# Attention scores as 64-row products, one per head, in place of 128-row products against a zero-padded query

## The chip, the cores and the metric

The kernel runs on one core of one Trainium2 chip. The metric is device time in microseconds, from one launch that computes the whole output. The core has a matrix engine (TensorE, PE in the profile), a vector engine (DVE), a scalar engine (ACT), a general engine (POOL), a queue engine (SP) and 16 DMA engines; each compute engine works through its own list of instructions in order and waits on semaphores for the others.

## The reference

Causal attention over 4 batches, 8 heads, 768 positions and 64 channels a head, followed by a gated feed-forward block. Heads 0, 2 and 6 see all earlier keys; the other five see the first four keys (the sinks) and the last 64.

```python
scores = (1.0 / np.sqrt(D)) * np.matmul(q, k.transpose(0, 1, 3, 2))      # (4, 8, 768, 768), D = 64
rel = pos[:, None] - pos[None, :]
full_mask   = rel >= 0
stream_mask = (rel >= 0) & ((pos[None, :] < 4) | (rel < 64))
a = softmax(where(mask of the head, scores, -1e9))
attn_out = np.matmul(a, v)
x = attn_out.transpose(0, 2, 1, 3).reshape(B * S, H * D)                 # (3072, 512)
g = x @ w_gate                                                           # (3072, 1536)
out = (g * sigmoid(g) * (x @ w_val)) @ w_out                             # (3072, 512)
```

## The kernel before

The 3072 positions are cut into 24 tiles of 128 query rows (`TILES`, six to a batch; a tile's number inside its batch is `i`, its place in the run is `t`). Keys and queries are brought to channel-major form: `kT` holds, for each block of 128 keys, two heads one above the other in the 128 partitions, 64 channels each. `PAIRS` lists which heads share a block: (0, 2), (4, 6), (1, 3), (5, 7). `qT` is held twice, once with the lower 64 partitions zero and once with the upper 64 zero (`fill` writes the zeros in `qT`, and in `hqz` for the pairs that a DMA transposes). A product over all 128 partitions with one of these halves gives the score of one head alone.

For each tile, `plan` lists units of up to eight score blocks of 128 keys by 128 queries. A block is a pair number `p`, the heads of the pair that are wanted, a column `c` in the unit's score buffer, and a key block `kt`. A block wanted for both heads is one product of 256 columns: one weight load of the 128 by 128 key block, then both zero-padded queries streamed through it. A block wanted for one head is a product of 128 columns. The first two units of a tile with `i >= 1` hold eight blocks each (the diagonal block, the block before it and the sink block, for all heads as needed); the remaining units hold the older key blocks of the three full heads, 3(i-1) blocks in all. A tile with `i == 0` has one unit of eight.

`scores` issues a unit's products into `sc`, a buffer of eight blocks in two banks of the matrix engine's output memory; there is one such buffer. `exps` takes the exponential of the unit on ACT into `e`. From tile `LEAD = 4` on, the causal and window masks are multiplied into `e` afterwards by `mask` (DVE or POOL) from the constant tiles `m0`, `m1`, `m2`, which `mask_fills` writes once from `FILLS`. In the first four tiles the masks are added in the products instead. `values` multiplies `e` with the values (`av`, 65 columns a product, the last one for the row sum), `recip` and `norm` divide, and the result is transposed into `xt` (`xtranspose`, on PE for the first eight tiles, by a DMA afterwards). `gate` runs the gate and value products of the feed-forward (`gv`, 512 columns a product, four of them to a result), `tanh`, `stt1` and `stt2` form the hidden tile `h`, and `outproj` multiplies by the output weights (`o_ps`). `store` writes the rows.

The work of all tiles and of the feed-forward is one list of tasks, each a few instructions. Which engine takes a task is written out in `WAYS`, and the order in which all tasks are issued is written out in `ORDER`, two characters to a task; no scheduler decides either when the kernel is built. The last lines of the kernel go through it:

```python
    for number in P.order():
        if number < P.FILL:
            P.tasks[number].run()
```

So a unit of scores (`sc t.u`) stands between whatever feed-forward, value or transposing products the list has beside it.

Of the kernel before, what the change touches and what calls it, by code (L numbers as in the profile page):

```python
# [9 lines left out]
AF = mybir.ActivationFunctionType  # L10
# [95 lines left out]
def kernel(  # L106
# [42 lines left out]
    scale = 1.0 / (D ** 0.5)  # L149
# [18 lines left out]
    def buf(ring, shape, dt, name):  # L168
        return pools[ring].tile(shape, dt, name=name, tag=ring)
# [9 lines left out]
    def recast(task, dst, src):  # L179
        if task.way == "DVE":  # L180
            nc.vector.tensor_reduce(out=dst, in_=src.unsqueeze(len(src.shape)),  # L181
                                    axis=mybir.AxisListType.X, op=ALU.max)
        else:
            copy(task, dst, src)
# [13 lines left out]
        out=ident, in_=ident, compare_op=ALU.not_equal, fill=1.0,  # L198
# [12 lines left out]
    DIAG, BAND0, OWN, FAR = range(4)  # L211

    m0 = const.tile([128, 8, 128], FH, name="m0")
    m1 = const.tile([128, 4, 128], FH, name="m1")
    m2 = const.tile([128, 5, 128], FH, name="m2")
# [28 lines left out]
    def mask_fill(task, dst, src):  # L244
        src = nat[:, src].unsqueeze(1).to_broadcast([128, dst.shape[1], 128])
        if task.way == "ACT":
            nc.scalar.activation(out=dst, in_=src, func=AF.Identity, scale=-1.0 / OFF, bias=1.0)
        else:
            nc.vector.tensor_scalar(out=dst, in0=src, scalar1=-1.0 / OFF, op0=ALU.mult,
                                    scalar2=1.0, op1=ALU.add)  # L250

    def mask_fills(x):
        def run():
            for dst, src in FILLS[x]:
                mask_fill(T_fill[x], dst, src)
        return run

    FILLS = [[(m0[:, 0:4], BAND0), (m0[:, 4:6], DIAG), (m0[:, 6:7], BAND0), (m0[:, 7:8], DIAG),
              (m2[:, 1:4], DIAG), (m2[:, 0:1], OWN), (m1[:, 0:2], OWN)],
             [(m2[:, 4:5], FAR), (m1[:, 2:4], FAR)]]  # L260

    kT = [const.tile([128, NT, 2, 2, 128], FH, name=f"kT{n}") for n in range(2)]
    qT = [const.tile([128, 2, 4, 2, 128], FH, name=f"qT{n}") for n in range(2)]
# [106 lines left out]
    LEAD = 4  # L370
# [89 lines left out]
    def sinks_v(b, m):  # L460
        V = vt[b % 2]
        for j in range(2):
            rows = slice(j * 64, j * 64 + NSINK // 2)
            recast(T_sv[b, m], V[rows, m, STREAMS], V[rows, 0, STREAMS])

    def plan(t):


        b, i = TILES[t]
        if i == 0:  # L470
            if t == 0:
                return [([(p, (0, 1), 2 * x, 0) for x, p in enumerate(ps)], 4, None)
                        for ps in ((2, 3), (0, 1))]
            return [([(p, (0, 1), 2 * x, 0) for x, p in enumerate((2, 3, 0, 1))], 8, m0)]
        if t == 1:
            return [([(p, (0, 1), 0, i), (p, (0, 1), 2, -1)], 4, None) for p in (2, 3)] + [
                ([(1, (0, 1), 0, i), (0, (0, 1), 2, i)], 4, None),
                ([(1, (0,), 0, -1), (1, (1,), 1, 0), (0, (0, 1), 2, 0)], 4, None)]
        us = [([(2, (0, 1), 0, i), (2, (0, 1), 2, -1), (3, (0, 1), 4, i), (3, (0, 1), 6, -1)],
               8, m1),  # L480
              ([(1, (0, 1), 0, i), (0, (0, 1), 2, i), (1, (0,), 4, -1), (1, (1,), 5, 0),
                (0, (0, 1), 6, 0)], 8, m2)]
        rest = [(0, (0, 1), kt) for kt in range(1, i)] + [(1, (1,), kt) for kt in range(1, i)]
        unit, at = [], 0
        for p, hh, kt in rest:
            if at + len(hh) > 8:
                us.append((unit, at, None))
                unit, at = [], 0
            unit.append((p, hh, at, kt))
            at += len(hh)  # L490
        if unit:
            us.append((unit, at, None))
        return us

    def marks(t, u):

        if t >= LEAD:
            return []
        if t == 0:
            return [[(0, BAND0, 4)], [(0, DIAG, 2), (2, BAND0, 1), (3, DIAG, 1)]][u]  # L500
        if t == 1:
            return [[(0, OWN, 2), (2, FAR, 2)], [(0, OWN, 2), (2, FAR, 2)],
                    [(0, OWN, 1), (1, DIAG, 3)], [(0, FAR, 1)]][u]
        if TILES[t][1] == 0:
            return [(0, BAND0, 4), (4, DIAG, 2), (6, BAND0, 1), (7, DIAG, 1)]
        if u == 0:
            return [(0, OWN, 2), (2, FAR, 2), (4, OWN, 2), (6, FAR, 2)]
        return [(0, OWN, 1), (1, DIAG, 3), (4, FAR, 1)]

    def block(t, p, kt):  # L510

        b, i = TILES[t]
        kt = i - 1 if kt < 0 else kt
        return kT[b % 2][:, kt, p % 2, p // 2]

    def value(t, h, kt):
        b, i = TILES[t]
        kt = i - 1 if kt < 0 else kt
        return vt[b % 2][:, kt, slot(h), 0:65]

    whole_sc, es, av_blocks = {}, {}, {}

    def score_ring(t, u):
        return "gv" if t < 2 and u % 3 else "sc"

    def scores(t, u, unit):
        if t < 2:
            sc = [buf(score_ring(t, u), [128, 4, 128], FP, "sc")]
            whole_sc[t, u] = sc[0]
        else:  # L530
            sc = whole_sc[t, u] = buf("sc", [128, 8, 128], FP, "sc")
            sc = [sc[:, 0:4], sc[:, 4:8]]
        half = slice(t % 2 * 64, t % 2 * 64 + 64)
        terms = [(c, n, ident, nat[:, m].unsqueeze(1).to_broadcast([128, n, 128]))
                 for c, m, n in marks(t, u)]
        terms += [(c, len(hh), block(t, p, kt), qT[t // 2 % 2][:, hh[0]:hh[-1] + 1, p, :, half])
                  for p, hh, c, kt in unit[0]]
        for c, n, weights, moving in terms:
            first, last = True, True
            if t < LEAD:  # L540

                in_bank = [x for x in terms if x[0] // 4 == c // 4]
                first, last = moving is in_bank[0][3], moving is in_bank[-1][3]
            nc.tensor.matmul(  # L544
                sc[c // 4][:, c % 4:c % 4 + n, :], weights, moving, start=first, stop=last)

    def exps(t, u, unit):
        e = es[t, u] = buf("e", [128, 8, 128], FH, "e")
        for p, hh, c, kt in unit[0]:
            for n, s_ in enumerate(hh):  # L550
                h = PAIRS[p][s_]
                av_blocks.setdefault((t, h), []).append((e[:, c + n, :], value(t, h, kt)))
        n = unit[1]
        nc.scalar.activation(  # L554
            out=e[:, 0:n], in_=whole_sc.pop((t, u))[:, 0:n], func=AF.Exp, scale=scale)

    def mask(task, t, u, m):
        ev, mm = es[t, u][:, 0:m.shape[1]], m
        if m is m1:
            ev = es[t, u].rearrange("p (g n) q -> p g (n q)", g=2)  # L560
            mm = m.rearrange("p n q -> p (n q)").unsqueeze(1).to_broadcast([128, 2, 512])
        ENG[task().way].tensor_tensor(out=ev, in0=ev, in1=mm, op=ALU.mult)  # L562
# [121 lines left out]
    def tasks_of_tile(t):  # L684
        b, i = TILES[t]
        units = plan(t)
        n = t // 2
        k_deps = [x for kt in range(i // 2 + 1) for x in T_ev[QP.index((b, kt)), 2]]
# [9 lines left out]
        for u, unit in enumerate(units):  # L698
            mms, nb, m = unit
            streams = any(kt < 0 or kt == i for p, hh, c, kt in mms if p)  # L700
            added = [T_masks[0 if t == 0 else 1]] if t < LEAD else []
            sc = P.add(f"sc{t}.{u}", ["PE"], (lambda t=t, u=u, unit=unit: scores(t, u, unit)),
                       deps=k_deps + k_sinks + added, takes=[score_ring(t, u)])
            T_sc_of[b, i].append(sc)
            if streams:
                own.append(sc)
            ex = P.add(f"ex{t}.{u}", ["ACT"], (lambda t=t, u=u, unit=unit: exps(t, u, unit)),
                       deps=[sc], takes=["e"])
            P.uses(sc, score_ring(t, u), ex)
            ms = []  # L710
            if m is not None and t >= LEAD:
                cell = []
                ms.append(P.add(f"mask{t}.{u}", ["DVE", "POOL"],
                                (lambda cell=cell, t=t, u=u, m=m:
                                 mask(lambda: cell[0], t, u, m)), deps=[ex] + T_fill))
                cell.extend(ms)
            for p, hh, c, kt in mms:
                for s_ in hh:
                    hd = heads.setdefault(PAIRS[p][s_], [set(), set()])
                    hd[0].update(ms or [ex])  # L720
                    hd[1].add(ex)
# [206 lines left out]
```

The softmax here doesn't subtract the row's maximum and nothing guards it: scores larger than these inputs give would overflow.

## Time and profile before

| what | us |
|---|---|
| runs of the kernel | 257.55, 256.27, 257.90; median 257.55 |
| span of the profiled execution | 255.7 |
| PE busy by the profile | 246.3 (96%) |
| DVE / ACT / POOL busy | 172.8 / 140.8 / 83.0 |
| score products against the keys, L544 | 276, of which 196 of 256 columns and 80 of 128 |
| feed-forward products, L775 and L810 | 608 and 300 |
| products with the values, L574 | 472 |

The time that the runs give is the whole execution; the profiled one shows a span of 255.7 us from its first to its last instruction, and the median of the runs lies 1.85 us above that span. In the rows of the profile, "128*128" names the part of the array that a product takes, "128x256 f16" the streamed operand. A product's recorded duration runs from its start to its modelled end, and the records of neighbouring products overlap; so the durations of products can't be added up, and the pace of the engine is read from one start to the next. "PEld" is the row of weight loads. "sc", "av", "gv", "o_ps" are buffers that the products write.

### The profile page before, as it was taken

How to read it: one execution, taken by the hardware profiler on the slowest of the kernel's cores; microseconds unless marked ns; L12 is line 12 of the kernel's file. 1: busy time of each engine (PE TensorE's matmuls, PEld its weight loads, DVE VectorE, ACT ScalarE, POOL GpSimd, SP SyncE). 2: the span in 40 equal slices, each digit the busy share in tenths (PEclk: the TensorE clock that was granted, in tenths of full speed). 3: DMA queues.
4: the chain of work that ended last, by engine and by line, in shares of the span. 5: the costliest groups of instructions: out<-in, count | busy, mean ns of one | idle time of the engine just before them, and what ended most of it. 6: DMA issues, size and time to landing. Idle time of an engine off the chain costs nothing.

```text
span 255.7 us, 4837 instructions
## 1 busy us (share of the span) xinstructions
PE 246.3 (96%) x1812; PEld 137.0 (54%) x1812; DVE 172.8 (68%) x356; ACT 140.8 (55%) x218; POOL 83.0 (32%) x117
## 2 busy tenths in 40 slices
PE   7988999999999999999999999999999999999993
PEld 3566766665555564545565555455545544444442
DVE  4888899986978666776858776579674656454610
ACT  2488788777857673567786725644526322223111
POOL 7366666996670160044164361005000000000000
PEclk9999999999999999999999999999999999999999
DMA  6999999969999999999964962571200233103124
GB/s 186 290 312 332 319 327 322 295 194 198 343 196 223 233 218 164 248 217 201 185 139 93 306 156 38 104 145 42 62 0 3 62 85 82 41 0 82 44 68 99
DMA packets 80535, 42.52 MB, mean 166 GB/s; under 512 B 32768, under 2 KB 76032, under 8 KB 80512
## 3 DMA queue, kind: packets, MB, share of 16 engines
q1 hardware_dynamic: 80352, 42.09, 69.5%
q8 instruction: 14, 0.23, 0.4%
q10 hardware_dynamic: 160, 0.13, 0.2%
q14 instruction: 9, 0.07, 0.1%
HBM read 28.31 MB, written 6.29 MB: 135 GB/s over the span
## 4 chain that ended last, share of the span: by engine, by line
PE 81%; DVE 11%; ACT 2%; issue 2%; DMA 2%; POOL 0%; DVEq 0%; POOLq 0%; ACTq 0%
PE gv L775 43%; PE o_ps L810 22%; PE sc L544 9%; PE av L574 4%; DVE h L792 2%; PE warm L291 2%; ACT e L554 2%; DVE vt L181 2%; DMA xt<-xb 2%; DVE sil L785 1%; DVE xb L591 1%; DVE e L562 1%; DVE qT L177 1%; DVE o_sb L177 1%; DVE rc L579 1%
## 5 line engine op out<-in xcount | busy, mean ns | idle before, releaser
L554 ACT ACTIVATE e<-sc 128x1024 f16<-128x1024 f32 (+3 forms) x71 | 62.1, 879 | 35.4 <-PE sc L544 34.6
L775 PE MATMUL gv<-xt,wv_sb 128*128 128x512 f16 (+1 forms) x304 | 72.6, 368 | 1.0 <-DVE sil L785 0.9
L775 PE MATMUL gv<-xt,wg_sb 128*128 128x512 f16 (+1 forms) x304 | 71.7, 368 | 0.6 <-DMA xt<-xb 0.3
L781 ACT ACTIVATE sig<-gv 128x512 f32<-128x512 f32 (+1 forms) x76 | 43.2, 574 | 51.3 <-PE gv L775 47.5
L810 PE MATMUL o_ps<-wo_sb,h 128*128 128x512 f16 (+2 forms) x300 | 69.5, 370 | 0.0
L785 DVE SCALAR_TENSOR_TENSOR sil<-sig,gv 128x512 f32<-128x512 f32 (+1 forms) x76 | 48.9, 655 | 28.6 <-ACT sig L781 27.7
L792 DVE SCALAR_TENSOR_TENSOR h<-sil,gv 128x512 f16<-128x512 f32 (+1 forms) x76 | 48.9, 655 | 18.9 <-PE gv L775 17.3
L775 PEld LDWEIGHTS <-wv_sb 128*128 128x128 f16 x304 | 28.7, 98 | 28.7 <-issue 2.0
L810 PEld LDWEIGHTS <-h 128*128 128x128 f16 x300 | 28.2, 98 | 29.1
L775 PEld LDWEIGHTS <-wg_sb 128*128 128x128 f16 x304 | 28.8, 98 | 27.5 <-issue 0.8
L544 PE MATMUL sc<-qT,kT 128*128 128x256 f16 (+1 forms) x276 | 37.4, 257 | 0.2 <-DVE qT L177 0.2
L562 POOL TENSOR_TENSOR e<-e,m 128x640 f16<-128x640 f16 (+1 forms) x15 | 26.4, 1768 | 14.9 <-ACT e L554 10.7
L544 PEld LDWEIGHTS <-kT 128*128 128x128 f16 x276 | 24.7, 98 | 12.0 <-issue 1.3
L574 PEld LDWEIGHTS <-e 128*128 128x128 f16 x472 | 19.7, 97 | 9.5 <-DVE xb L591 1.8
L574 PE MATMUL av<-vt,e 128*128 128x65 f16 x472 | 21.8, 193 | 0.9 <-DVE xb L591 0.6
L591 DVE TENSOR_TENSOR xb<-av,rc 128x256 f16<-128x256 f32 x48 | 20.2, 423 | 1.5
L579 DVE RECIPROCAL rc<-av 128x4 f32<-128x4 f32 x48 | 8.4, 177 | 14.0 <-PE av L574 13.7
L175 ACT COPY o_sb<-o_ps 128x512 f32<-128x512 f32 (+1 forms) x15 | 8.7, 578 | 16.2 <-PE o_ps L810 16.1
L562 DVE TENSOR_TENSOR e<-e,m 128x1024 f16<-128x1024 f16 (+1 forms) x23 | 15.6, 678 | 0.3 <-ACT e L554 0.2
L177 POOL CAST vt<-raw 64x512 f16<-64x512 f32 x21 | 13.1, 625 | 7.1 <-DMA raw<-in_v_dram 6.4
L177 POOL COPY vt<-vt 2x330 f16<-2x330 f16 x14 | 7.1, 504 | 21.9 <-PE av L574 17.5
L177 POOL CAST hq<-raw 128x1024 f16<-128x1024 f32 (+1 forms) x11 | 11.2, 1020 | 7.4 <-DMA raw<-in_q_dram 4.2
(51 smaller groups left out, 135.6 us busy)
## 6 DMA issues: line engine op xcount, KB each, us to landing
raw<-in_q_dram SPq DMA_DIRECT2D x12, 512.0 KB, 6.6
raw<-in_k_dram SPq DMA_DIRECT2D x12, 512.0 KB, 6.8
raw<-in_v_dram SPq DMA_DIRECT2D x12, 512.0 KB, 7.3
out_dram<-o_sb SPq DMA_DIRECT2D x46, 128.0 KB, 2.4
raw<-in_moe_w_gate_dram SPq DMA_DIRECT2D x6, 512.0 KB, 8.1
raw<-in_moe_w_val_dram SPq DMA_DIRECT2D x6, 512.0 KB, 7.9
raw<-in_moe_w_out_dram SPq DMA_DIRECT2D x6, 512.0 KB, 6.2
xt<-xb SPq DMA_TRANSPOSE x16, 2.5
```

What stands on the lines that cost most here:

```text
L177: ENG[task.way].tensor_copy(out=dst, in_=src)
L544: nc.tensor.matmul(sc[c // 4][:, c % 4:c % 4 + n, :], weights, moving, start=first, stop=last)
L554: nc.scalar.activation(out=e[:, 0:n], in_=whole_sc.pop((t, u))[:, 0:n], func=AF.Exp, scale=scale)
L562: ENG[task().way].tensor_tensor(out=ev, in0=ev, in1=mm, op=ALU.mult)
L574: nc.tensor.matmul(av[:, n, 0:65], ee, vv, start=(m == 0), stop=(m == len(bl) - 1))
L579: nc.vector.reciprocal(out=rc, in_=avs[t, odd][:, :, 64:65])
L591: nc.vector.tensor_tensor(out=xbs[t][:, :, odd, :], in0=av[:, :, 0:64], in1=rc.to_broadcast([128, 4, 64]), op=ALU.mult)
L775: nc.tensor.matmul(ps, wsb[:, kk, j * 128:(j + 1) * 128], xt[:, kk, c[0]:c[1]], start=(kk == 0), stop=(kk == 3))
L781: nc.scalar.activation(out=sg[g, j, c], in_=gs[g, j, c], func=AF.Tanh, scale=0.5)
L785: nc.vector.scalar_tensor_tensor(out=sl[g, j, c], in0=sg.pop((g, j, c)), scalar=1.0, op0=ALU.add, in1=gs.pop((g, j, c)), op1=ALU.mult)
L792: nc.vector.scalar_tensor_tensor(out=hs[g, j][:, c[0]:c[1]], in0=sl.pop((g, j, c)), scalar=0.5, op0=ALU.mult, in1=vs.pop((g, j, c)), op1=A ...
L810: nc.tensor.matmul(o_open[g, tt, x], hs[g, j][:, tt * 128:(tt + 1) * 128], wo_sb[:, j, lo:hi], start=(j == 0), stop=(j == NJ - 1))
```

## The change

From the fifth tile on (`t >= LEAD`), `plan` hands over to a new function `halves`. Every block of a unit becomes a product of its own, with 64 contracted rows: the 64 partitions of its head in `kT` as weights (64 by 128), and the same 64 partitions of the query that is not zero, 128 columns. In the units, upper rows (head 0 of the pair) and lower rows (head 1) alternate; blocks of the upper rows go to columns 0 to 3 of the score buffer, which is one bank, blocks of the lower rows to columns 4 to 7, the other bank. Units keep their number, and each keeps its place in `ORDER` and its engine in `WAYS`.

The older key blocks are cut differently: two key blocks (six score blocks) to a unit, then the rest. In tiles with `i == 4` this makes units of six and three in place of eight and one, with `i == 5` six and six in place of eight and four. In those units two upper products stand against four lower ones, or one against two. A unit that doesn't start at column 0 is read by `exps` from its first used column on. The masks are laid out anew to match: `m2` is applied from column 1, and `FILLS` has the same number of writes with other slices. The zeros of `qT` and `hqz` are still written, though the new products don't read them. The first four tiles are unchanged.

```diff
-    FILLS = [[(m0[:, 0:4], BAND0), (m0[:, 4:6], DIAG), (m0[:, 6:7], BAND0), (m0[:, 7:8], DIAG),
-              (m2[:, 1:4], DIAG), (m2[:, 0:1], OWN), (m1[:, 0:2], OWN)],
-             [(m2[:, 4:5], FAR), (m1[:, 2:4], FAR)]]
+    FILLS = [[(m0[:, 0:2], BAND0), (m0[:, 3:6], BAND0), (m0[:, 2:3], DIAG), (m0[:, 6:8], DIAG),
+              (m2[:, 2:5], DIAG), (m2[:, 1:2], OWN), (m1[:, 0:2], OWN)],
+             [(m2[:, 0:1], FAR), (m1[:, 2:4], FAR)]]
...
+    def halves(i):
+
+        if i == 0:
+            return [([(p, (s_,), 4 * s_ + x, 0) for x, p in enumerate((2, 3, 0, 1))
+                      for s_ in range(2)], 8, m0)]
+        us = [([(p, (s_,), 4 * s_ + x, kt) for x, (p, kt) in enumerate(
+                  ((2, i), (3, i), (2, -1), (3, -1))) for s_ in range(2)], 8, m1),
+              ([(0, (0,), 0, 0), (0, (1,), 5, i), (1, (0,), 1, -1), (1, (1,), 4, i),
+                (1, (0,), 2, i), (1, (1,), 6, 0), (0, (0,), 3, i), (0, (1,), 7, 0)], 8, m2)]
+        kts = list(range(1, i))
+        for ks in (kts[:2], kts[2:]):
+            unit = []
+            for x, kt in enumerate(ks):
+                unit += [(0, (0,), 4 - len(ks) + x, kt), (0, (1,), 4 + 2 * x, kt),
+                         (1, (1,), 5 + 2 * x, kt)]
+            if unit:
+                us.append((unit, 4 + 2 * len(ks), None))
+        return us
+
     def plan(t):
         b, i = TILES[t]
+        if t >= LEAD:
+            return halves(i)
...
-        terms += [(c, len(hh), block(t, p, kt), qT[t // 2 % 2][:, hh[0]:hh[-1] + 1, p, :, half])
-                  for p, hh, c, kt in unit[0]]
+        if t < LEAD:
+            terms += [
+                (c, len(hh), block(t, p, kt), qT[t // 2 % 2][:, hh[0]:hh[-1] + 1, p, :, half])
+                for p, hh, c, kt in unit[0]]
+        else:
+            for p, hh, c, kt in unit[0]:
+                rows = slice(hh[0] * 64, hh[0] * 64 + 64)
+                terms.append((c, 1, block(t, p, kt)[rows],
+                              qT[t // 2 % 2][rows, hh[0]:hh[0] + 1, p, :, half]))
...
-        n = unit[1]
+        at = slice(min(c for _, _, c, _ in unit[0]), unit[1])
         nc.scalar.activation(
-            out=e[:, 0:n], in_=whole_sc.pop((t, u))[:, 0:n], func=AF.Exp, scale=scale)
+            out=e[:, at], in_=whole_sc.pop((t, u))[:, at], func=AF.Exp, scale=scale)
...
-        ev, mm = es[t, u][:, 0:m.shape[1]], m
+        at = 1 if m is m2 else 0
+        ev, mm = es[t, u][:, at:at + m.shape[1]], m
```

## The prediction

> **What bounds the kernel now.** I read the page's busy shares and slices first, then what PE waited for, then PE's rows by form, then single stretches of its timeline.
>
> ```profile
> PE 246.3 (96%) x1812; PEld 137.0 (54%) x1812; DVE 172.8 (68%) x356; ACT 140.8 (55%) x218; POOL 83.0 (32%) x117
> ...
> PE   7988999999999999999999999999999999999993
> ...
> DVE  4888899986978666776858776579674656454610
> ACT  2488788777857673567786725644526322223111
> ...
> PEclk9999999999999999999999999999999999999999
> DMA  6999999969999999999964962571200233103124
> ```
>
> PE is at nine tenths in nearly every slice at the full clock; DVE and DMA come close only early. Busy PE could still be a PE with gaps, so the next view is PE's waits from 52 us to the end:
>
> ```profile
> PE gv L775 <- DVE sil L785: 0.3, 1, 0.3
> PE gv L775 <- DMA xt<-xb: 0.3, 1, 0.3
> PE gv L775 <- DVE h L792: 0.2, 1, 0.2
> ```
>
> That is 0.8 us in over 200. From 52 us on, every nanosecond that PE's stream gains or loses is a nanosecond of the kernel, with no other engine to hide it. PE's rows by form, and two stretches of its timeline (start, length, what):
>
> ```profile
> L775 PE MATMUL gv<-xt,wv_sb 128*128 128x512 f16 x272 | 67.8, 379 | 0.3 <-DVE sil L785 0.3
> L544 PE MATMUL sc<-qT,kT 128*128 128x256 f16 x196 | 33.8, 272 | 0.2 <-DVE qT L177 0.2
> L574 PE MATMUL av<-vt,e 128*128 128x65 f16 x472 | 21.8, 193 | 0.9 <-DVE xb L591 0.6 <-ACT e L554 0.3
> L544 PE MATMUL sc<-qT,kT 128*128 128x128 f16 x80 | 11.0, 219 | 0.0
> ```
>
> ```profile
> 104.13 0.59 PE L775 MATMUL gv<-xt,wv_sb 128*128 128x512 f16 x2
> 104.56 0.60 PE L544 MATMUL sc<-qT,kT 128*128 128x256 f16 x5
> 105.00 1.03 PE L810 MATMUL o_ps<-wo_sb,h 128*128 128x512 f16 x4
> 105.87 0.38 PE L775 MATMUL gv<-xt,wv_sb 128*128 128x512 f16 x1
> ```
>
> Four products of 512 columns take 105.87 - 105.00 = 0.87 us, 216 ns each, while each record lasts 379: a tail of 163 ns that overlaps the successor. The score unit of five products takes 0.44 us from its start to the next, and lasts 0.60: the same tail. Per 128 columns the pace is 216 / 4 = 54, with a little for each product; start to start I take 56 for 128 columns and 109 for 256. The unit above, three of 256 and two of 128, then takes 3 x 109 + 2 x 56 = 439 ns, as seen. Neither entering nor leaving it costs anything, and the weight loads (98 ns each in the rows) are all hidden. What an unhidden one costs is seen where a wait holds it up:
>
> ```profile
> 97.64 0.98 PEld L775 LDWEIGHTS <-wg_sb 128*128 128x128 f16 x6 [0.80 <-DMA xt<-xb]
> 97.65 1.25 PE L775 MATMUL gv<-xt,wg_sb 128*128 128x512 f16 x5 [0.30 <-DMA xt<-xb]
> ```
>
> Product starts 0.01 us after load; I take 15 ns for a load with nothing in front of it.
>
> **What the Trainium skill says.** "TensorEngine Tiling (Array Packing)", Key Properties: tiles of 64 by 128 load weights and multiply in parallel, but changing the tiling mode, not just the tile, drains the engine; no price is given. The same page, Gotcha 1: different row tiles must write different banks, which the change observes. "TensorE: Matmul & The Clock Gate", Part 3: products in different row groups start about 4 ns apart. Its Part 2 puts the drain through the array at about 128 cycles behind the last column; at the 128 columns in about 54 ns read above, that is an estimate of 53 ns. The trace of before shows none of this: every product in it is "128*128". It shows only the unbroken pace and the 163 ns tail.
>
> **The change part by part.** *Scores removed and added.* By the plans, the first four tiles keep 26 of the 276 products (22 of 256 columns, 4 of 128). The other twenty lose 196 - 22 = 174 of 256 and 80 - 4 = 76 of 128: 174 x 109 + 76 x 56 = 23.2 us of PE. They gain 424 products of 128 columns over 64 rows, in 62 units: 38 of eight (two for each of 18 tiles, one for each of 2), 16 of six, 8 of three. If an upper and a lower product run beside each other, a unit of eight takes 4 slots of 56 ns, one of six 4 (four lower against two upper), one of three 2: 152 + 64 + 16 = 232 slots, 13.0 us. Saved 10.2 us, or 165 ns a unit. Twice as many weight loads come with it, two in each slot of 56 ns; at 15 each they fit. Bounds for a slot: 56 ns (fully parallel) to 112 (two products one after the other, then 424 x 56 = 23.7 us, nothing saved). I take 56: the page says parallel, and banks and order are laid out for it.
>
> *Switches added.* In PE's order all 62 units stand alone: before each comes a product over 128 rows and after each another (mostly gv, then av and o_ps). So there are 124 changes of mode. Bounds for one: zero, if the drain is not real or is hidden; 53 + 15 = 68 ns if only the array must run empty and then a load is exposed; 163 + 15 = 178 ns if the whole tail seen in the rows must pass before the next load. Below zero nothing speaks for. I take the middle of the last two, 123 ns: a drain must at least empty the array, and the tail holds read and write latencies that may or may not be waited for. 124 x 0.123 = 15.3 us. That falls on PE, which has no slack to hide it from 52 us on (48 of the 62 units); of the 14 before, a little may fall into waits that PE has there anyway.
>
> *Exponentials, masks, fills, order.* ACT reads the same number of columns in the same 62 instructions, in other groups (768 and 384 for 1024 and 128); the masks have the same shapes and the fills the same count. DVE, POOL, SP and the DMAs issue the same work in the same places: nothing. Cover isn't needed.
>
> *Sum.* -10.2 + 15.3 = +5.1 us on the profiled execution, 255.7 to 260.8 of span; with the 1.85 us that the median lies above the span, 262.6 us, 2.0% slower.
>
> **The rivals.**
>
> *Free switches (the other side).* If a switch costs under 82 ns (10.2 us / 124) the kernel gets faster, and under 61 by more than 1%. At zero, PE saves 10.2 us, of which 2.3 (14 units of 165 ns) lie before 52 us, where DVE is busy 24.3 of the 26 us from 26 to 52 (the view by windows) and takes the place of PE. Of the other 7.9 I keep 6: until 130 us the DMAs are busy without a break, and the one wait of PE on a transposing DMA would grow. 251.5 us. For it: the trace shows PE going between plain products and transposing ones at the usual pace, so not every change costs. Against: the page's drain.
>
> *Only the array empties.* 68 ns: 8.4 - 10.2 = -1.8 us, 255.8 us, no measurable change.
>
> *The whole tail.* 178 ns: 22.1 - 10.2 = +11.9 us, 269.4 us. For it: the tail is the one latency that the rows do show.
>
> *No pairing: the change doesn't do what it says.* If the halves run one after the other, 424 x 56 ns is 0.5 us more than before, and the switches come on top: +0.5 + 15.3, 273.3 us; with a free switch, 258. Against: separate banks and alternating rows.
>
> **How the numbers follow.** Something near the middle price, slower by 1 to 3.5%: 0.36. Whole tail, slower still: 0.20. No pairing: 0.12, nearly all slower. Only the array: 0.10. Free: 0.22. So slower by over 1% is 0.67, within 1% (about what a measurement of this kernel can tell from no change) 0.11, faster by over 1% 0.22. The likeliest case is 262.6, its own range 260.2 (103 ns a switch) to 267. The wide range reaches to 250 on the free side and 273 on the other; below it lies a saving that the early part and the DMAs hardly allow, above it the dearer half of no pairing.
>
> **What would show it.** Right: in the timeline a unit of eight lasts about 224 ns from its first to its last slot, with pairs of starts a few ns apart; before its first product and before the first product after it, an idle stretch of about 100 ns that no semaphore explains, so "issue" time on PE or PEld grows by some 15 us; ACT, DVE and POOL keep their busy times. Wrong: starts at an even 56 ns in a unit (no pairing); units entered and left at the usual pace (free switches); or weight loads in a unit that start only when the product before has ended (the slot is longer than 56). If PE's waits on DVE or DMA grow by several us in a faster kernel, the gain was capped as I assumed.

## The result, and the profile after

The changed kernel takes 258.95 us (median) where the kernel before, run beside it, takes 257.29 us: a ratio of 1.0067, with a 95% interval of 1.0041 to 1.0093. That is 1.7 us slower (1.1 to 2.4), clear of no change, and a third of the 5.1 us that were forecast. The profiled execution has a span of 256.2 us, only 0.5 above that of before. It is one of the quicker ones of its kernel (258.00 us against the median of 258.95), so times are compared by medians below; the profile shows the mechanism and how long PE's products and switches take.

From the page of the changed kernel: busy times, PE's slices, and the groups of the score products and of their weight loads.

```profile
PE 248.0 (97%) x1986; PEld 125.7 (49%) x1986; DVE 172.1 (67%) x356; ACT 141.0 (55%) x218; POOL 81.9 (32%) x117
...
PE   7888999999999999999999999999999999999993
...
PEclk9999999999999999999999999999999999999999
...
L572 PE MATMUL sc<-qT,kT 64*128 64x128 f16 (+2 forms) x450 | 27.8, 222 | 0.3 <-DVE qT L177 0.3
L572 PEld LDWEIGHTS <-kT 64*128 64x128 f16 (+1 forms) x450 | 15.5, 94 | 20.6 <-issue 19.2
```

DVE, ACT and POOL have what they had. PE shows 174 more products. What is new is in the last line: weight loads of the scores stand behind 19.2 us in which nothing that the profile shows held them up ("issue"), where the same group of before had 1.3 us. That is not yet the price: before each such load the stretch also holds the time of the product that is still running, in the unit below 0.42 us, of which 0.09 is lost. So a growth of 17.9 us, near the 15 that the prediction named as its sign, does not confirm its price.

How a unit of eight looks from outside, first PE, then PEld (start, length, what):

```profile
103.74 0.38 PE L804 MATMUL gv<-xt,wv_sb 128*128 128x512 f16 x1
...
104.05 0.10 PEld L572 LDWEIGHTS <-kT 64*128 64x128 f16 x2 [0.42 <-issue]
```

```profile
104.05 0.40 PE L572 MATMUL sc<-qT,kT 64*128 64x128 f16 x8
104.38 1.04 PE L839 MATMUL o_ps<-wo_sb,h 128*128 128x512 f16 x4
105.25 1.03 PE L804 MATMUL gv<-xt,wv_sb 128*128 128x512 f16 x4
```

The product of 512 columns at 103.74 would have made room after 216 ns, at 103.96. The first weight load of the unit, and with it the first product, comes at 104.05: 0.09 us later, with no semaphore in the profile to explain it. The unit itself is eight products in 104.38 - 104.05 = 0.33 us, of which 4 slots of 56 ns are 0.22 and nearly all of the rest is the way out. From the end of the 512-column slot to the next full-array product it takes 104.38 - 103.96 = 0.42 us. The unit of five products shown for the kernel before took 0.44. The pairs have halved the time of the products, and the two changes of mode have taken nearly all of it back.

The starts of the single records give the parts, with the same values in all 62 units to a few ns. A pair starts 3 to 4 ns apart. The wait before the first product is 95 to 96 ns over the usual pace, whether 512, 256, 128 or 65 columns went before. The second pair of the unit comes about 10 ns late, the first full-array product 92 ns, and the one behind it 10 more. One way in and one way out: about 210 ns.

A unit of six in the changed kernel, and a unit of the kernel before that held the same work (two products for two heads, two for one):

```profile
119.02 0.59 PE L804 MATMUL gv<-xt,wg_sb 128*128 128x512 f16 x2
119.55 0.40 PE L572 MATMUL sc<-qT,kT 64*128 64x128 f16 x6
119.88 0.42 PE L603 MATMUL av<-vt,e 128*128 128x65 f16 x8
```

```profile
119.91 0.49 PE L544 MATMUL sc<-qT,kT 128*128 128x256 f16 x4
120.24 0.22 PE L574 MATMUL av<-vt,e 128*128 128x65 f16 x2
```

Before: 0.33 us, with no price at either end. After: the second 512-column product starts at 119.24 and is through at 119.45; from there to 119.88 is 0.43 us, 0.10 more than before. A unit of six takes as long as one of eight, because four lower products need four slots whatever stands beside them. That is where the loss should be; two of the experiments test it.

### The profile page after: what moved, and what is told of

It reads as the page before. It is cut to its first block, busy times and chain, and to the rows that moved or that the text cites. A ratio compares the mean times of both kernels' runs of the same rounds, so it can differ in the third digit from the quotient of the medians.

```text
span 256.2 us, 5179 instructions
## 1 busy us (share of the span) xinstructions
PE 248.0 (97%) x1986; PEld 125.7 (49%) x1986; DVE 172.1 (67%) x356; ACT 141.0 (55%) x218; POOL 81.9 (32%) x117
## 4 chain that ended last, share of the span: by engine, by line
PE 91%; DVE 4%; ACT 2%; issue 0%; POOL 0%; POOLq 0%; DVEq 0%
PE gv L804 49%; PE o_ps L839 25%; PE sc L572 9%; PE av L603 6%; ACT e L582 2%; PE warm L291 2%; DVE vt L181 1%; PE xtr L636 1%; PE tr L435 1%; DVE h L821 1%; DVE xb L620 1%; DVE qT L177 1%; DVE m L249 0%; PE tr L432 0%; DVE sil L814 0%
## 5 line engine op out<-in xcount | busy, mean ns | idle before, releaser
L839 PEld LDWEIGHTS <-h 128*128 128x128 f16 x300 | 27.4, 98 | 30.0
L804 PEld LDWEIGHTS <-wv_sb 128*128 128x128 f16 x304 | 27.5, 98 | 29.2 <-issue 0.9
L804 PEld LDWEIGHTS <-wg_sb 128*128 128x128 f16 x304 | 27.5, 98 | 28.3 <-issue 0.3
L572 PE MATMUL sc<-qT,kT 64*128 64x128 f16 (+2 forms) x450 | 27.8, 222 | 0.3 <-DVE qT L177 0.3
L572 PEld LDWEIGHTS <-kT 64*128 64x128 f16 (+1 forms) x450 | 15.5, 94 | 20.6 <-issue 19.2
L603 PEld LDWEIGHTS <-e 128*128 128x128 f16 x472 | 19.3, 97 | 10.2 <-DVE xb L620 2.0
L591 DVE TENSOR_TENSOR e<-e,m 128x1024 f16<-128x1024 f16 (+1 forms) x23 | 14.5, 630 | 0.3 <-ACT e L582 0.2
L177 POOL CAST vt<-raw 64x512 f16<-64x512 f32 x21 | 12.8, 610 | 5.2 <-DMA raw<-in_v_dram 4.6
```

Of the source, the lines that this page charges most:

```text
L177: ENG[task.way].tensor_copy(out=dst, in_=src)
L572: nc.tensor.matmul(sc[c // 4][:, c % 4:c % 4 + n, :], weights, moving, start=first, stop=last)
L603: nc.tensor.matmul(av[:, n, 0:65], ee, vv, start=(m == 0), stop=(m == len(bl) - 1))
L804: nc.tensor.matmul(ps, wsb[:, kk, j * 128:(j + 1) * 128], xt[:, kk, c[0]:c[1]], start=(kk == 0), stop=(kk == 3))
L839: nc.tensor.matmul(o_open[g, tt, x], hs[g, j][:, tt * 128:(tt + 1) * 128], wo_sb[:, j, lo:hi], start=(j == 0), stop=(j == NJ - 1))
```

## The experiments

All ratios are to the kernel before, run beside them on the same chip. The "stream" is PE's work from the trace: every product at its usual pace from start to start, plus the delays at the changes of mode, without PE's other waits; 234.4 us for the kernel before, from its first score product on.

**Full rows.** The new plan and masks without the mode.

```diff
-                rows = slice(hh[0] * 64, hh[0] * 64 + 64)
+                rows = slice(0, 128)
```

> The changed plan, units, masks and order, but every single-head product takes all 128 rows against the zero-padded query (no 64-row mode, no pairing). Theory (the cost is the switches of mode): PE's stream of scores is 424 x 56 ns = 23.7 us, 0.5 us over that of the kernel before, so a ratio to before of about 1.002 (0.999 to 1.004). Rival (the loss comes from the new grouping of exponentials and masks, not from PE's mode): it stays at the changed kernel's 1.007.

Measured: 256.93 us against 256.72, ratio 1.0004 (0.9991 to 1.0017). The new units, masks and exponentials cost nothing that can be seen. The loss belongs to the 64-row products.

**Pairs in the units of eight only.** `halves` gives the first two units of a tile, the old plan the rest.

```diff
-        if t >= LEAD:
+        if t >= LEAD and i == 0:
             return halves(i)
...
+        if t >= LEAD:
+            us = halves(i)[:2]
...
-        if t < LEAD:
+        if t < LEAD or u >= 2:
             terms += [
```

> 64-row pairs only in the 38 units of eight that are the first two of a tile; the older key blocks keep the old plan and 128 rows. Theory (each unit pays about 207 ns for entering and leaving, a unit of eight saves 213): nothing gained, nothing lost, ratio 0.999 (0.996 to 1.002). Rival (the loss is the same in each of the 62 units): 38/62 of 0.7%, ratio 1.004.

Measured: 257.27 against 256.72, ratio 1.0012 (0.9999 to 1.0025). Within the theory's range, though above its 0.999; the rival's 1.004 is excluded.

**Pairs in the older key blocks only.** The reverse, built on the kernel before.

```diff
+        if t >= LEAD:
+            return us + halves(i)[2:]
...
+        if t < LEAD or u < 2:
             terms += [
```

> 64-row pairs only in the units of older key blocks (16 of six, 8 of three); the first two units of each tile stay at 128 rows. Theory: 24 units pay 207 ns each and save 106 or 53, together with the new cut 9.45 us of PE for 6.6, +2.85 us less what early waits take up: ratio 1.008 to 1.011. Rival (same loss in each unit): 24/62 of 0.7%, ratio 1.003.

Measured: 258.21 against 256.72, ratio 1.0060 (1.0042 to 1.0078). The 24 units that save least by pairing carry nearly all of the loss; the rival's 1.003 is excluded. The theory's 1.008 to 1.011 lies above the interval as well: the stream did grow by 3.0 us, near the 2.85 expected, but only 1.5 us of it were measured (see the table below).

**A full pair in the middle, or at the end.** Two kernels: one of the four pairs of each unit of eight takes 128 rows, the third or the last.

```diff
-            for p, hh, c, kt in unit[0]:
+            for n, (p, hh, c, kt) in enumerate(unit[0]):
                 rows = slice(hh[0] * 64, hh[0] * 64 + 64)
+                if len(unit[0]) == 8 and n in (4, 5):        # the control: (6, 7)
+                    rows = slice(0, 128)
```

> The changed kernel, but in each of the 38 units of eight the third pair takes 128 rows (zero-padded query), between pairs of 64 rows: two switches of mode more in each unit. Theory (a switch costs about 104 ns wherever it stands): 38 x (56 for the lost pairing + 207) = 10.0 us over the changed kernel, ratio 1.037 to 1.046. Rival (the price hangs on the long products around a unit, not on the switch): 38 x 56 ns = 2.1 us, ratio 1.015, as with the full pair at the end.

> Control: the same full pair, but as the last of the unit, so the number of switches is that of the changed kernel. Both theories: 38 x 56 ns = 2.1 us over the changed kernel, ratio 1.013 to 1.016.

Measured: 268.71 against 257.09, ratio 1.0461 (1.0423 to 1.0498) with the full pair in the middle; 259.77, ratio 1.0123 (1.0075 to 1.0170) with it at the end. That is the upper end of what the theory said for the first, and just under what both said for the second; the rival's 1.015 for the first is excluded. The two kernels have the same numbers of products of each form, only the place of the full pair in the unit differs, and so 76 changes of mode: 8.9 us, or 118 ns for each by the difference of the medians. By the traces the streams differ by 8.0 us, 106 each. Timelines, the middle first:

```profile
109.82 0.67 PE L574 MATMUL sc<-qT,kT 64*128 64x128 f16 x8
110.42 1.04 PE L841 MATMUL o_ps<-wo_sb,h 128*128 128x512 f16 x4
```

```profile
104.73 0.56 PE L574 MATMUL sc<-qT,kT 64*128 64x128 f16 x8
105.13 1.03 PE L841 MATMUL o_ps<-wo_sb,h 128*128 128x512 f16 x4
```

0.60 us and 0.40 us for eight products each (a group is named after its first record). A change of mode inside a unit, with no long product near it, costs what one at its edge costs.

**Every unit twice.** The products of each unit from the fifth tile on are issued a second time over the first.

```diff
+        if t >= LEAD:
+            terms = terms + terms
         for c, n, weights, moving in terms:
```

> The changed kernel, with every unit's 64-row products issued twice in a row, the second time over the first: same switches, double the work inside the mode. Theory (pairs in parallel at 56 ns): 232 x 56 ns = 13.0 us over the changed kernel, less what early waits take up: ratio 1.047 to 1.058. Rival (pairing is only partial, the switches cheaper than the trace suggests): up to 23.7 us, ratio up to 1.099.

> The kernel before, with every unit's 128-row products from the fifth tile on issued twice in a row. Theory: 23.2 us over before, less what early waits take up: ratio 1.080 to 1.091. Against the doubled 64-row kernel this gives the saving inside the mode without the switches: 10.2 us if pairs run fully in parallel, near 0 if they don't.

Measured: 271.51 against 257.09, ratio 1.0567 (1.0528 to 1.0605), for the changed kernel doubled, which is 12.8 us more than the changed kernel's own ratio: 232 slots of 55 ns. The kernel before, doubled: 277.70, ratio 1.0810 (1.0772 to 1.0849), 20.8 us. Both lie in the ranges of the theory. The doubled unit in 64 rows:

```profile
111.07 0.62 PE L574 MATMUL sc<-qT,kT 64*128 64x128 f16 x16
111.62 0.61 PE L841 MATMUL o_ps<-wo_sb,h 128*128 128x512 f16 x2
```

Sixteen products in 0.55 us, against 0.33 for eight: 0.22 for four more slots. Pairing is complete. The saving inside the mode comes to 23.2 - 13.0 = 10.2 us by the streams in the table below, and to 20.8 - 12.8 = 8.0 by the medians, each of which is uncertain by about 1 us. And with units twice as long the sign turns: the 64-row kernel is 6.2 us faster than the 128-row one with the same doubled work.

**Upper rows first, lower rows after.**

```diff
-            for p, hh, c, kt in unit[0]:
+            for p, hh, c, kt in sorted(unit[0], key=lambda x: x[1]):
```

> The changed kernel, but inside each unit all upper-row products first, then all lower-row ones; same banks, same switches. Theory (PE starts products in order and pairs only neighbours): a unit of eight takes 7 slots of 56 ns for 4, one of six 5 for 4: 38 x 168 + 16 x 56 = 7.3 us more, ratio about 1.035 (1.027 to 1.036). Rival (PE pairs across its queue whatever the order): 1.007.

Measured: 259.28 against 256.72, ratio 1.0083 (1.0057 to 1.0109). The theory was wrong here, the rival right: 7.3 us were expected over the changed kernel, and 0.4 came.

```profile
105.05 0.41 PE L572 MATMUL sc<-qT,kT 64*128 64x128 f16 x8
105.39 0.39 PE L839 MATMUL o_ps<-wo_sb,h 128*128 128x512 f16 x1
```

Eight products in 0.34 us again, though the four upper ones are issued ahead of the four lower ones. In the single records starts come in pairs 13 to 14 ns apart, in place of 3 to 4. Seven slots and the way out would have been 0.49 us. The records don't say which rows a product took, so this is a conclusion: if two products can't share the same rows, PE started lower products before upper ones that were issued earlier and waited for their rows. Each engine was said above to work through its list in order; for PE's products on different rows that doesn't hold here.

**Early tiles, late tiles.** The forecast held that the 14 units before 52 us could hide a little. Two kernels take full rows in all tiles but 4 to 7, or in those alone.

```diff
                 rows = slice(hh[0] * 64, hh[0] * 64 + 64)
+                if t >= 8:                                   # the other kernel: t < 8
+                    rows = slice(0, 128)
```

> The changed plan and order; 64-row products only in tiles 4 to 7, whose 14 units stand before 52 us; later tiles take all 128 rows. Against the kernel with full rows everywhere (ratio 1.000) PE's stream grows by 8 x -17 + 4 x 95 + 2 x 151 ns = 0.55 us. Theory (the waits that PE has on DVE in this part take it up): ratio 1.000 to 1.001. Rival (nothing is taken up): 1.0025.

> The reverse: tiles 4 to 7 take all 128 rows, the 48 units from tile 8 on take 64-row pairs. PE's stream grows by 30 x -17 + 12 x 95 + 6 x 151 ns = 1.54 us against full rows everywhere. Theory: nearly all of it is seen, ratio 1.004 to 1.0065, close to the changed kernel's 1.0067. Rival (the early units carry their share of the loss): 1.004 or less, and early and late together make up the whole.

Measured: 257.63 against 256.85, ratio 1.0020 (1.0001 to 1.0038) for the early tiles; 258.62, ratio 1.0069 (1.0042 to 1.0095) for the late ones. The early result fits the rival better and does not exclude the theory's 1.001; the late one lies just above the theory's range, which its interval overlaps. Undecided: the intervals are as wide as the difference asked for.

**All of them together.** Growth over the kernel before, in us: the stream by the trace, and the median by the ratio.

| kernel | stream | measured |
|---|---|---|
| full rows | +0.4 | +0.1 |
| units of eight only | -0.1 | +0.3 |
| early tiles only | +1.1 | +0.5 |
| late tiles only | +2.3 | +1.8 |
| older key blocks only | +3.0 | +1.5 |
| changed kernel | +2.9 | +1.7 |
| upper first, lower after | +3.5 | +2.1 |
| full pair at the end | +5.1 | +3.2 |
| full pair in the middle | +13.1 | +11.9 |
| 64-row units twice | +15.9 | +14.6 |
| 128-row units twice | +23.2 | +20.8 |

The stream carries every row, but where it grows by over 1 us, 0.5 to 2.4 us of it don't arrive. So PE's waits must have become shorter. Over the whole run, the longest wait of the feed-forward products in the kernel before (first block; the 0.3 us for the DMA and the 0.2 for `h` shown with the prediction are the others), and all of PE's waits in the changed kernel (second):

```profile
PE gv L775 <- DVE sil L785: 0.9, 3, 0.4
```

```profile
PE warm L291 <- POOL ident L197: 1.4, 1, 1.4
PE sc L572 <- ACT e L582: 0.9, 4, 0.2
PE av L603 <- DVE xb L620: 0.6, 2, 0.4
PE sc L572 <- DVE qT L177: 0.3, 1, 0.3
PE av L603 <- ACT e L582: 0.3, 1, 0.3
PE xtr L636 <- DVE xt L177: 0.3, 1, 0.3
PE tr L432 <- ACT hq L175: 0.2, 1, 0.2
```

All 1.4 us of waits of the feed-forward products, counted against modelled ends, are gone. By starts, PE's waits from its first score product on sum to 7.1 us before, 4.9 in the changed kernel and 4.0 with the 128-row units twice. But these are single executions, and they alone don't show that the slower stream is the reason: in the one of full rows, whose stream is only 0.4 us longer, this is left:

```profile
PE gv L804 <- DVE sil L814: 0.2, 1, 0.2
```

All twelve traces together show it for the part from 52 us on (from the same feed-forward product in each). Counted by starts, PE's waits there are 0.9 to 1.7 us in the four kernels whose stream grows by 0.4 us or less in that part (before, full rows, units of eight only, early tiles only), and 0.2 to 0.4 us in seven of the eight whose stream grows there by 2.2 us or more (0.7 in the eighth, older key blocks only). Before 52 us there is no such order: the wait of one `gv` product near 40 us is 0.2 us in the profiled execution of the changed kernel and 1.1 in that of late tiles only. So from 52 us on a slower PE finds about 0.8 us of waits already over; where the rest of the shortfall lies is not settled.

## Why the prediction was right or wrong

Slower was right; 5.1 us were forecast and 1.7 measured, below the range of the likeliest case. Two steps failed, the size of a switch and the slack.

*The bound.* Right. PE's stream sets the time, and all eleven kernels follow it to within the waits of the table.

*The saving of 10.2 us.* Right by the stream. Pairs run at 56 ns a slot, and the doubled kernels confirm it: 232 slots gave 12.8 us, the doubled 128-row products 20.8 of the 23.2 in the stream. The four slots of a unit with four lower and two upper products were right too.

*Switches.* That they cost was right, shown by the full pair in the middle against one at the end. That all 62 units pay in and out, with nothing at the unit's edge to hide it, was right too, by the starts in the trace. The size failed. The step took 123 ns, the middle between an emptied array (68) and the whole tail (178). The trace shows 96 + 10 on the way in and 92 + 10 on the way out, with a few ns in the unit: 13.2 us in all, 106 ns for each of 124, where 15.3 were summed. Nothing in the trace of before spoke for the middle rather than for either end, and the result is a small difference of two near equal terms: an error of 17 ns a switch is 2.1 us of the forecast 5.1. What the 92 to 96 ns at an edge consist of is not shown.

*No slack from 52 us on.* This failed as well: the stream grew by 2.9 us and the median by 1.7, 1.2 less (0.5 to 1.8 by the interval). The 0.8 us of waits after 52 us were read as "no slack to hide it", but they are waits that a later PE need not make, and by the traces about 0.8 us came back there. A stretch in which PE hardly waits is not one without anything to give back. The other 0.4 us lie before 52 us, where the prediction allowed for a little, or in the spread of the runs. Together the two make up the miss, 5.1 - 2.1 - 1.2 = 1.8 us; the 1.2 is what is left between stream and median, not a measurement of its own.

*Exponentials, masks, fills.* Right: full rows, ratio 1.0004.

*The rivals.* No pairing: excluded. Free switches: excluded. Array alone (68 ns) and whole tail (178 ns): both excluded by the 106 ns of a switch in the trace, 92 to 96 of them idle PE at the edge. The time fell into the case "within 1%", but not for the reason that this rival gave: the switch was dearer than 68, and than the 82 at which nothing is lost or gained, and waits gave part of the loss back.

*What the pages stated.* The Trainium skill, "TensorEngine Tiling (Array Packing)", Key Properties, says that a change of mode drains the engine; the idle 92 to 96 ns at each change agree with that. Its page "TensorE: Matmul & The Clock Gate", Part 3, gives about 4 ns between the starts of a pair, and the trace shows 3 to 4. The same part says that products start in strict order without reordering; the kernel with the upper rows first shows eight products in four slots, so here the measurement differs, unless two products shared the same rows, and decides.

## What to carry to other kernels

A pair of 64-row products of 128 columns takes 56 ns here, half of the same work against a zero-padded operand, but each stay in that mode costs about 210 ns of PE's time, in and out. So count stays first, then the products in each: a stay pays only when pairing saves more than that, which in this kernel means units of eight break even, units of six or three lose, and units of twice the length, as in the doubled kernels, gain. When a forecast is a small difference of two large terms, price the unknown one with a kernel of its own before trusting the sign, and count waits of the bounding engine as something that a slower stream may give back.

## What the runs showed of the hardware that was not expected

- The wait at a change of mode does not depend on what went before: 95 to 96 ns over the pace behind products of 512, 256, 128 and 65 columns, 92 on the way out.
- Issued four upper, then four lower, eight products still ran in four slots of 56 ns, with starts 13 to 14 ns apart: such a unit took 340 ns from its start to the next full-array product, where the alternating one took 330. By this, PE takes products for the two row halves independently; alternating rows in the program was hardly needed.
- Whether the two halves need separate banks was not tried, nor 64-row products of another width than 128 columns.
